# Full-width FFN, weight and angle products given out as four 32-column matmuls

## The chip, the core and the metric

The kernel runs on one core of a Trainium2 chip. A core has five engines with queues of their own: TensorE (PE, matrix products, with its weight loads shown as PEld), VectorE (DVE), ScalarE (ACT), GpSimd (POOL) and SyncE (SP, which here only issues DMAs). Each engine takes its instructions in the order of the program and waits on semaphores where it needs another's result. The metric is device time in microseconds, lower is better. All data are 32-bit floats.

## What is computed

A gated linear recurrence per head, and then a feed-forward block whose hidden layer is the largest of three products:

```python
for t in range(S):                                    # S = 768, B = 4, H = 8, D = 48
    S_re, S_im = ar*S_re - ai*S_im + kv, ar*S_im + ai*S_re
    y[:, :, t] = np.einsum('bhd,bhde->bhe', q[:, :, t], S_re)
x = y.transpose(0, 2, 1, 3).reshape(3072, 384)
h = np.maximum(np.maximum(x @ w1, x @ w2), x @ w3)    # w1..w3: 384 x 768
return h @ w_out                                      # w_out: 768 x 384
```

`ar` and `ai` are the gates `a_re` and `a_im` after they are scaled to a magnitude of at most 0.999.

## The kernel before

The 3072 rows are 24 blocks `x` of 128 steps; a group `g` (0 to 11) holds two of them, x and y, one of each of two batches. For each group the kernel works out the gates with logarithms (`gates`), sums angles along time with a triangular matrix (`cs`), sums logarithms (`sums`, `F`), turns k and q, transposes them (`tp`), forms scores (`A`, `B`), the state (`dk`), and outputs (`y`). The outputs of a group are the moving operand of the FFN: first three products by w1, w2, w3 (`up` for a whole group, 256 rows at a time; `up_one` for one block of the first two), then the product by w_out (`op`). For whole groups that last product is built from seven smaller ones, a Strassen scheme (`seven`), with 192 moving columns each, and two products with 384 (`Px`, `Py`). `project` makes it in the plain way for the first two blocks. `product` multiplies two weight matrices once, near the start (`wm`).

The whole order of work is written out by hand in the string `SCHEDULE`: a word such as `U11:3` or `P5:4` names a step and a group, and `Bound` (line 201 is its call) ties each instruction of an engine behind the engine's previous one. So the profile gives line 201 for nearly everything, and tiles are told apart by their names. No scheduler moves anything. PSUM is used as four pairs of banks, which the string `SLOTS` shares out in turn.

Every matrix product is `lhsT` (stationary, its columns become output partitions) by `rhs` (moving, its columns are streamed). In the trace each product of the program stands as two pairs of weight load and matmul (a transpose as one pair): 5,436 products of the program, 786 of them transposes, are the 10,086 matmuls of the profile. What part of the array a product takes is its shape, rows by columns:

- 128 x 128: `up`, `op` (from `up`, `up_one`, `seven`, `project`), `wm`, and, untouched by the change, `wt` and `pw` near the start.
- 128 x 64: `cs`, two products side by side on two column halves.
- 128 x 32: `A`, `B` and `y`, four side by side on the four column quarters (A and B use 112 of the rows).
- 64 x 64: `dk`, `F`, `sums`. 64 rows by 128: `tp`.

The products of one shape that follow each other are called a block below.

The calls that matter, before the change: `mm(out=ps[:, j], lhsT=ws[i][:, d, b*P:(b+1)*P], rhs=features(g)[:, ...])` in `up` (128 stationary columns, 256 moving), the same with `factor(i)` in `seven` (192 moving), `wx[:, 0]` for `Px`, `Py` and `wo`, `wp` in `project` (384 moving).

Of the kernel before, what the change touches and what calls it, by code (L numbers as in the profile page):

```python
# [139 lines left out]
def kernel(  # L140
# [15 lines left out]
    P = 128  # L156
    L64 = 64
# [30 lines left out]
    T = {}  # L188
# [18 lines left out]

    pe, dve, act, pool, sp = (Bound(e) for e in (nc.tensor, nc.vector, nc.scalar, nc.gpsimd, nc.sync))
    mm = pe.matmul

    def banks(nm, n=None):

# [182 lines left out]
    def every(view, j):  # L395

        return view.rearrange("p (i u d) -> p i u d", u=2, d=D)[:, :, j]
# [55 lines left out]
    def product(name, f):  # L453

        third = (vbs[2].rearrange("p c i d -> p (c i d)"), vbs[3].rearrange("p c i d -> p (c i d)"),
                 us["k"][2].rearrange("p h d -> p (h d)"))[f][:, 0:2 * DM]
        if name == "T":
            ps = T["wt", f] = banks("wt", 2 * DM)
            for u in range(2):
                for d in range(KD):  # L460
                    o = u * DM + d * P
                    pe.transpose(out=ps[:, o:o + P], in_=ws[0][:, d, (2 * f + u) * P:(2 * f + u + 1) * P], identity=ident)
        elif name == "t":
            act.copy(out=third, in_=T["wt", f])
        elif name == "M":
            for d in range(KD):
                ps = once(("wm", d // 2), lambda: banks("wm"))[:, d % 2, 0:DM]
                for u in range(2):
                    mm(out=ps, lhsT=third[:, u * DM + d * P:u * DM + (d + 1) * P], rhs=wo[:, 2 * f + u],
                       start=2 * f + u == 0, stop=2 * f + u == KF - 1)  # L470
        elif f < 2:
            n = 2 - f
            activation(out=wp[:, 2 * f:2 * f + n], in_=T["wm", f][:, 0:n, 0:DM], func=AF.Copy, scale=-1.0)
# [108 lines left out]
    def angles(g, c, name):  # L582

        x = g * C + c
        if name == "cs":
            ps = T["cs", x] = banks("cs", DM)
            for ch in range(2):
                for j in range(2):
                    dst, m = ps[j * L64:(j + 1) * L64, ch * HC:(ch + 1) * HC], slice(ch * L64, (ch + 1) * L64)
                    mm(out=dst, lhsT=upto[:, m], rhs=every(T["w", g][:, c * DM:(c + 1) * DM], j), start=True, stop=True)  # L590
        elif name == "t":
            T["t", x] = turned["t"][c]
            activation(out=T["t", x], in_=T["cs", x], func=AF.Copy, scale=-1.0, bias=MAGIC)
        elif name == "nf":
            T["nf", x] = turned["nf"][c]
            dve.scalar_tensor_tensor(out=T["nf", x], in0=T["t", x], scalar=MAGIC, in1=T["cs", x],
                                     op0=OP.subtract, op1=OP.add)
        elif name == "Cd":
            if (g + 1) % NS > 0:
                t = flat(T["ar", g + 1])[0:1]  # L600
                for j in range(2):
                    last = (j + 1) * L64
                    pool.dma_start(out=every(t[:, c * DM:(c + 1) * DM], j), accum_op=OP.add,
                                   in_=T["nf", x][last - 1:last, HC:].rearrange("p (i d) -> p i d", d=D))
        elif name == "af":
            T["af", x] = turned["t"][c]
            magnitude(T["af", x], T["nf", x])
        elif name in ("sa", "sb"):
            CS = T["CS", x] = css[c]
            if name == "sa":  # L610
                activation(out=CS[:, :, 0], in_=hv(T["af", x]), func=AF.Sin, scale=TWOPI, bias=-0.5 * math.pi)
            else:
                activation(out=CS[:, :, 1], in_=hv(T["nf", x]), func=AF.Sin, scale=TWOPI)
        else:
            return False
        return True
# [214 lines left out]
    def features(g):  # L831

        return xhx[:, 0:KD] if g % 2 == 0 else xhx[:, KD + KF:]
# [3 lines left out]
    def up_one(key, f, i, name):  # L837

        if name == "U":
            ps = T["up1", key, f, i] = banks("up", 2 * P).rearrange("p (f t) -> p f t", t=P)  # L840
            for j in range(2):
                for d in range(KD):
                    mm(out=ps[:, j], lhsT=ws[i][:, d, (f * 2 + j) * P:(f * 2 + j + 1) * P],
                       rhs=T["xT", key][:, d], start=(d == 0), stop=(d == KD - 1))
            return
        ps = T["up1", key, f, i]
        hT = once(("hT", key), lambda: ld2.tile([P, KF, P], FP, tag="ar", name="hT"))
        larger(hT[:, f * 2:(f + 1) * 2], ps, i)
# [9 lines left out]
    def up(g, f, i, name):  # L858

        if name == "U":  # L860
            ps = T["up", g, f, i] = banks("up", 3 * TG).rearrange("p (f t) -> p f t", t=TG)
            for j in range(3):
                b = ALONG[g % 2][3 * f + j]
                for d in range(KD):
                    mm(out=ps[:, j], lhsT=ws[i][:, d, b * P:(b + 1) * P],
                       rhs=features(g)[:, (d + 2 * (g % 2)) % KD], start=(d == 0), stop=(d == KD - 1))
        else:
            larger(xhx[:, KD + 3 * f:KD + 3 * f + 3], T["up", g, f, i], i)

# [23 lines left out]
    def seven(g, name):  # L893

        a11, a12, a21, a22 = (split(c, half, g) for c in range(2) for half in range(2))
        s1, s2, s3 = (sums[:, i] for i in range(3))
        if name in ("S1", "S2", "S3", "S4"):
            out, in0, in1, op = {"1": (s1, a21, a22, OP.add), "2": (s2, s1, a11, OP.subtract),
                                 "3": (s3, a11, a21, OP.subtract), "4": (s1, a12, s2, OP.subtract)}[name[1]]
            dve.tensor_tensor(out=out, in0=in0, in1=in1, op=op)  # L900
            return
        if name in ("P1", "P5", "P6", "P7", "r1", "r6", "r75", "r57"):
            ps = once(("seven", g), lambda: banks("op"))
            r = {1: ps[:, 0, 0:NH], 6: ps[:, 0, NH:DM], 5: ps[:, 1, 0:NH], 7: ps[:, 1, NH:DM]}
        else:
            ps = once(("op7", g), lambda: banks("op"))
            r = {2: ps[:, 0, 0:NH], 3: ps[:, 0, NH:DM], 4: ps[:, 1, 0:NH]}
        if name[0] == "P" and name[1:].isdigit():
            i = int(name[1:])
            left = {1: a11, 2: a12, 3: s1, 4: a22, 5: s1, 6: s2, 7: s3}[i]  # L910
            for n in range(4):
                mm(out=r[i], lhsT=left[:, n], rhs=factor(i)[:, (n + 2 * (g % 2)) % 4],
                   start=i in (1, 5, 6, 7) and n == 0, stop=i != 2 and n == 3)
        elif name in ("Px", "Py"):
            c = "xy".index(name[1])
            x0 = features(g)[:, 2 * (g % 2), c * P:(c + 1) * P]
            mm(out=ps[:, c, 0:DM], lhsT=x0, rhs=wx[:, 0], start=True, stop=False)
        else:
            ot = ots
            xl, xr, yl, yr = (ot[:, c, h * NH:(h + 1) * NH] for c in range(C) for h in range(2))  # L920
            if name == "r1":
                act.copy(out=xl, in_=r[1])
            else:
                if name == "r75":
                    two_ = ot.rearrange("p c n -> p (c n)")[:, NH:3 * NH].rearrange("p (u n) -> p u n", u=2)
                    again = yl.rearrange("p (u n) -> p u n", u=1).to_broadcast([P, 2, NH])
                    dve.tensor_tensor(out=two_, in0=again, in1=ps[:, 1, 0:DM].rearrange("p (u n) -> p u n", u=2), op=OP.add)
                    return
                out, in0, in1 = {"r6": (yl, xl, r.get(6)), "r57": (yr, yl, r.get(5)),
                                 "ox": (ot[:, 0], ot[:, 0], ps[:, 0, 0:DM]),  # L930
                                 "oy": (ot[:, 1], ot[:, 1], ps[:, 1, 0:DM])}[name]
                for n in (slice(NH, DM), slice(0, NH)) if name == "oy" and g == NG - 1 else (slice(None),):
                    dve.tensor_tensor(out=out[:, n], in0=in0[:, n], in1=in1[:, n], op=OP.add)

    def project(x, name):

        if name == "O":
            ps = T["op", x] = banks("op", DM)
            for d in range(KD):
                mm(out=ps, lhsT=T["xT", x][:, d], rhs=wp[:, d], start=(d == 0), stop=False)  # L940
            for f in range(KF):
                mm(out=ps, lhsT=T["hT", x][:, f], rhs=wo[:, f], start=False, stop=(f == KF - 1))
        elif name == "o":
            act.copy(out=ots[:, x % C], in_=T["op", x])
        elif name == "D":
# [97 lines left out]
```

## Time and profile before

| what | value |
|---|---|
| time, median of 3 runs | 559.99 us (558.49 to 560.16) |
| profiled execution: span, first to last instruction | 553.2 us |
| PE busy | 523.6 us (95%), 10,086 matmuls |
| DVE busy | 482.1 us (87%) |
| ACT busy | 368.2 us (67%) |
| POOL busy | 70.8 us (13%) |
| mean granted TensorE clock | 0.992 |

The profile gives for each engine the busy time, and for a group of instructions its count, its busy time, the mean duration of one and the idle time before it. A matmul's duration holds its way through the array, and matmuls overlap, so durations do not add up; what a matmul costs is the step from one to the next. The chain of waits follows the work back from the last instruction: each piece is the time from the end of the piece before it to its own end, with the number of instructions in it. For PE such a piece is what the block added to the end.

### The profile page before, as it was taken

The numbers are of one execution on the slowest core, as the hardware profiler recorded it, in microseconds if no ns is written. First come the engines' busy times: TensorE is split into PE (matmuls) and PEld (weight loads), VectorE is DVE, ScalarE is ACT, GpSimd is POOL, SyncE is SP. The second block draws the span as 40 slices with busy tenths as digits, with TensorE's granted clock in tenths as the row PEclk, the third lists the DMA queues.
The fourth block names the chain that finished last, engine by engine and source line by source line (L and its number), as shares of the span: only waits on it lengthen the run. The fifth ranks groups of instructions, "written<-read, shape, count | busy, mean of one in ns | idle before, by whom it ended". The sixth has DMA issues, their size and how long they took to land.

```text
span 553.2 us, 22687 instructions
## 1 busy us (share of the span) xinstructions
PE 523.6 (95%) x10086; PEld 448.1 (81%) x10086; DVE 482.1 (87%) x752; ACT 368.2 (67%) x653; POOL 70.8 (13%) x113
## 2 busy tenths in 40 slices
PE   2669799999999999999999999999999999999996
PEld 1355697788888888888988988988988988898985
DVE  4999999999999997999988888999999998887432
ACT  7999987777867787868776768786637835520100
POOL 7224140030020020000210200120020020000000
PEclk9979999999999999999999999999999999999999
DMA  8989774262616332324353245542361153000000
GB/s 203 295 246 176 174 131 79 50 128 63 109 38 124 67 68 51 61 44 88 72 121 58 35 85 108 101 91 54 62 125 20 32 105 72 2 31 2 31 1 28
DMA packets 141953, 47.51 MB, mean 86 GB/s; under 512 B 130464, under 2 KB 135584, under 8 KB 141856
## 3 DMA queue, kind: packets, MB, share of 16 engines
q1 hardware_dynamic: 136272, 37.77, 31.5%
q0 software_dynamic: 5584, 8.30, 8.9%
q8 instruction: 79, 1.29, 1.0%
q14 instruction: 18, 0.15, 0.1%
HBM read 33.03 MB, written 4.72 MB: 68 GB/s over the span
## 4 chain that ended last, share of the span: by engine, by line
PE 84%; DVE 7%; ACT 4%; SPq 2%; issue 1%; DMA 1%; DVEq 0%; ACTq 0%
PE up L201 33%; PE op L201 24%; PE y L201 7%; PE A L201 5%; PE tp L201 4%; PE dk L201 3%; PE sums L201 2%; PE cs L201 2%; DVE w L201 2%; SPq L201 2%; PE F L201 2%; PE B L201 1%; DMA wo<-in_moe_w_dram 1%; DVE atm L201 1%; ACT f L201 1%
## 5 line engine op out<-in xcount | busy, mean ns | idle before, releaser
L201 PE MATMUL up<-xhx,w 128*128 128x256 f32 x792 | 177.0, 382 | 0.1
L201 PEld LDWEIGHTS up<-xhx,w 128*128 128x128 f32 x792 | 148.6, 190 | 21.5 <-PE B L201 0.3
L201 ACT ACT_TABLE_LOAD x49 | 62.9, 1283 | 1.6 <-PEq L1027 0.8
L201 ACT COPY atm<-B 32x128 f32<-32x128 f32 x96 | 24.6, 256 | 37.8 <-DVE atm L201 19.7
L201 PE MATMUL op<-wo,xhx 128*128 128x192 f32 (+1 forms) x220 | 48.4, 363 | 0.0
L201 DVE TENSOR_TENSOR Q<-Q,f 112x1024 f32<-112x1024 f32 (+1 forms) x48 | 45.4, 952 | 1.7 <-ACT Q L201 1.2
L201 POOL DMA_DIRECT2D ar<-nf x40 | 34.6, 1305 | 60.3 <-DVE ar L201 48.9
L201 ACT ACTIVATE f<-F 48x232 f32<-48x232 f32 x96 | 34.5, 359 | 10.1 <-PE F L201 6.1
L201 PEld LDWEIGHTS op<-wo,xhx 128*128 128x128 f32 x220 | 36.5, 190 | 4.6 <-issue 0.6
L201 PE MATMUL y<-atm,vb 128*32 128x64 f32 x1152 | 39.0, 221 | 0.2 <-ACT K L201 0.2
L201 PE MATMUL y<-QG,g 112*32 112x64 f32 x1408 | 38.0, 219 | 0.2 <-issue 0.2
L201 PEld LDWEIGHTS y<-atm,vb 128*32 128x32 f32 x1152 | 32.4, 109 | 5.3 <-issue 2.9
L201 PEld LDWEIGHTS y<-QG,g 112*32 112x32 f32 x1408 | 34.8, 109 | 0.3 <-issue 0.3
L201 DVE TENSOR_TENSOR ot<-ot,op 128x384 f32<-128x384 f32 (+1 forms) x56 | 25.6, 464 | 10.7 <-PE op L201 6.4
L201 PE MATMUL op<-wo,strassen 128*128 128x192 f32 x176 | 33.0, 331 | 0.0
L201 POOL DMA_DIRECT2D Ln<-e x9 | 8.3, 923 | 192.2 <-ACT e L201 53.8
L201 PE MATMUL A<-Q,K 112*32 112x80 f32 x1536 | 31.6, 234 | 1.4 <-DVE Q L201 1.4
L201 DVE COPY_PREDICATED atm<-masko,A 128x256 f32<-128x256 uint8 x72 | 31.2, 435 | 1.7
L201 PE MATMUL op<-w,strassen 128*128 128x192 f32 x176 | 32.2, 329 | 0.0
L201 PEld LDWEIGHTS A<-Q,K 112*32 112x32 f32 x1536 | 27.3, 110 | 4.2 <-issue 3.1
L201 PEld LDWEIGHTS op<-wo,strassen 128*128 128x128 f32 x176 | 28.8, 190 | 0.8
L201 ACT COPY Q<-tp 112x1024 f32<-112x1024 f32 x22 | 22.3, 1014 | 10.7 <-PE tp L201 10.5
(148 smaller groups left out, 1080.5 us busy)
## 6 DMA issues: line engine op xcount, KB each, us to landing
ar<-in_a_re_dram SPq DMA_DIRECT2D x24, 192.0 KB, 3.1
ai<-in_a_im_dram SPq DMA_DIRECT2D x24, 192.0 KB, 3.5
q<-in_q_dram SPq DMA_DIRECT2D x96, 48.0 KB, 2.6
k<-in_k_dram SPq DMA_DIRECT2D x96, 48.0 KB, 2.6
vb<-in_v_dram SPq DMA_DIRECT2D x96, 48.0 KB, 3.0
out_dram<-ot SPq DMA_DIRECT2D x23, 192.0 KB, 2.6
Ln<-e POOLq DMA_DIRECT2D x9, 384.0 KB, 4.1
w<-L POOLq DMA_DIRECT2D x7, 384.0 KB, 4.4
```

Source lines behind the costliest of these rows:

```text
L201: ins = f(*a, **kw)
```

## The change

A helper `mmq` gives a product out as four, one for each quarter of 32 stationary columns, with the same moving operand. `up`, `up_one`, `seven` (`P1` to `P7`, `Px`, `Py`), `project` and the weight product in `product` call it in place of `mm`. `cs` goes from two 64-column products per half to four with 32 columns. What is computed, the order of the steps, the tiles, and the instructions of the other engines stay as they are. SP's DMAs keep their order; three loads of v wait for one more semaphore of PE or ACT than before.

```diff
+    def mmq(out, lhsT, rhs, **kw):
+
+        for o in range(0, P, 32):
+            mm(out=out[o:o + 32], lhsT=lhsT[:, o:o + 32], rhs=rhs, **kw)
...
-                    mm(out=ps, lhsT=third[:, u * DM + d * P:u * DM + (d + 1) * P], rhs=wo[:, 2 * f + u],
-                       start=2 * f + u == 0, stop=2 * f + u == KF - 1)
+                    mmq(out=ps, lhsT=third[:, u * DM + d * P:u * DM + (d + 1) * P], rhs=wo[:, 2 * f + u],
+                        start=2 * f + u == 0, stop=2 * f + u == KF - 1)
...
-                for j in range(2):
-                    dst, m = ps[j * L64:(j + 1) * L64, ch * HC:(ch + 1) * HC], slice(ch * L64, (ch + 1) * L64)
-                    mm(out=dst, lhsT=upto[:, m], rhs=every(T["w", g][:, c * DM:(c + 1) * DM], j), start=True, stop=True)
+                for o in range(0, P, 32):
+                    dst, m = ps[o:o + 32, ch * HC:(ch + 1) * HC], ch * L64 + o % L64
+                    mm(out=dst, lhsT=upto[:, m:m + 32], rhs=every(T["w", g][:, c * DM:(c + 1) * DM], o // L64),
+                       start=True, stop=True)
...
-                    mm(out=ps[:, j], lhsT=ws[i][:, d, b * P:(b + 1) * P],
-                       rhs=features(g)[:, (d + 2 * (g % 2)) % KD], start=(d == 0), stop=(d == KD - 1))
+                    mmq(out=ps[:, j], lhsT=ws[i][:, d, b * P:(b + 1) * P],
+                        rhs=features(g)[:, (d + 2 * (g % 2)) % KD], start=(d == 0), stop=(d == KD - 1))
...
-                mm(out=r[i], lhsT=left[:, n], rhs=factor(i)[:, (n + 2 * (g % 2)) % 4],
-                   start=i in (1, 5, 6, 7) and n == 0, stop=i != 2 and n == 3)
+                mmq(out=r[i], lhsT=left[:, n], rhs=factor(i)[:, (n + 2 * (g % 2)) % 4],
+                    start=i in (1, 5, 6, 7) and n == 0, stop=i != 2 and n == 3)
...
-            mm(out=ps[:, c, 0:DM], lhsT=x0, rhs=wx[:, 0], start=True, stop=False)
+            mmq(out=ps[:, c, 0:DM], lhsT=x0, rhs=wx[:, 0], start=True, stop=False)
...
-                mm(out=ps, lhsT=T["xT", x][:, d], rhs=wp[:, d], start=(d == 0), stop=False)
+                mmq(out=ps, lhsT=T["xT", x][:, d], rhs=wp[:, d], start=(d == 0), stop=False)
             for f in range(KF):
-                mm(out=ps, lhsT=T["hT", x][:, f], rhs=wo[:, f], start=False, stop=(f == KF - 1))
+                mmq(out=ps, lhsT=T["hT", x][:, f], rhs=wo[:, f], start=False, stop=(f == KF - 1))
```

`up_one` is changed as `up` is. The program has 834 full-width products (396 and 72 `up` with 256 and 128 moving columns, 308 and 40 `op` with 192 and 384, 18 `wm` with 384) that become 3,336, and 96 `cs` that become 192: 2,598 products more, or 5,196 matmuls and as many weight loads in the trace.

More of the change, by code (lines that the diff above doesn't have):

```diff
@@ L842, in up_one @@
                 for d in range(KD):
-                    mm(out=ps[:, j], lhsT=ws[i][:, d, (f * 2 + j) * P:(f * 2 + j + 1) * P],
-                       rhs=T["xT", key][:, d], start=(d == 0), stop=(d == KD - 1))
+                    mmq(out=ps[:, j], lhsT=ws[i][:, d, (f * 2 + j) * P:(f * 2 + j + 1) * P],
+                        rhs=T["xT", key][:, d], start=(d == 0), stop=(d == KD - 1))
             return
```

## The prediction

> **What bounds the kernel now.** I read the busy times and the chain of waits on the page first.
>
> ```profile
> span 553.2 us, 22687 instructions
> PE 523.6 (95%) x10086; PEld 448.1 (81%) x10086; DVE 482.1 (87%) x752; ACT 368.2 (67%) x653; POOL 70.8 (13%) x113
> ...
> PE 84%; DVE 7%; ACT 4%; SPq 2%; issue 1%; DMA 1%; DVEq 0%; ACTq 0%
> PE up L201 33%; PE op L201 24%; PE y L201 7%; PE A L201 5%; PE tp L201 4%; PE dk L201 3%; PE sums L201 2%; PE cs L201 2%; DVE w L201 2%; SPq L201 2%; PE F L201 2%; PE B L201 1%; DMA wo<-in_moe_w_dram 1%; DVE atm L201 1%; ACT f L201 1%
> ```
>
> TensorE ends the kernel: 84% of the chain is its work, 59% of the span `up`, `op` and `cs`, the products that the change touches. The question is what a block of products costs PE. The chain in order of time tells it, since a piece is the time from the end of the block before to the block's own end:
>
> ```profile
> 59.49 1.75 DVE Q L201 x2
> 61.37 1.35 PE A L201 x64
> ...
> 116.39 4.08 PE up L201 x18
> ...
> 158.60 11.85 PE up L201 x54
> ...
> 263.04 2.80 PE op L201 x16
> ...
> 385.59 1.50 PE op L201 x8
> ```
>
> Up to about 62 us, while loads and gates are made, the chain runs through DVE and ACT (the `Q` of DVE above is the end of that); behind it 94% of the pieces' time are PE's, by the same view from 62 us on:
>
> ```profile
> by line: PE up L201 37.2%; PE op L201 26.8%; PE y L201 7.8%; PE A L201 5.4%; PE tp L201 4.4%; PE dk L201 3.8%; PE sums L201 2.7%; PE cs L201 2.6%; PE F L201 1.7%; PE B L201 1.7%; DVE atm L201 0.7%; issue 0.6%; DVE w L201 0.6%; ACT f L201 0.
> ```
>
> Thirty-six matmuls more of `up` take 11.85 - 4.08 = 7.77 us, so a step is 215.8 ns with 256 moving columns. Eight more of `op` take 1.30 us, a step of 162.5 ns with 192 columns. The difference, 53.3 ns for 64 columns, makes 0.833 ns a column. But 18 steps of 215.8 ns are 3.88 us, and the piece has 4.08; 8 steps of 162.5 ns are 1.30, and the piece has 1.50. Each full-width block, whatever its length, costs 0.20 us beyond its stream. That is what the change can remove.
>
> The same subtraction for the narrow shapes:
>
> ```profile
> 85.36 0.80 PE cs L201 x8
> ...
> 121.52 1.25 PE A L201 x64
> ...
> 127.65 0.39 PE B L201 x32
> 128.04 1.15 PE A L201 x64
> ...
> 139.37 1.45 PE cs L201 x16
> ...
> 186.49 1.73 PE y L201 x112
> 188.22 1.11 PE A L201 x64
> ```
>
> `cs`: eight more take 0.65 us, 162.5 ns for each two side by side, and 0.80 - 0.65 = 0.15 us go on the block itself. `A`, four side by side with 80 columns: 64 take 1.11 us right behind `y`, which has the same shape, so 69 ns for four, and 1.25 us behind `tp`, another shape. So coming from another shape costs 0.14 us, coming from the same shape nothing. This is the main reading: the 0.20 and 0.15 us are paid for the change of shape, not for the block.
>
> **The change part by part.** *The stream.* A full-width matmul with 80 columns would take 162.5 - 112 x 0.833 = 69.2 ns by the steps above. Four matmuls of `A` on the quarters take 69 ns. A `cs` pair with 192 columns takes 162.5 ns, as one `op` matmul with 192. So the fours and pairs that the trace has run side by side without loss, and I cost four quarters in place of one full width at nothing. [...] The trace shows no quarter with more than 80 columns, so the price has bounds. Below, 0: a four has the same columns to stream, and nothing in the rows streams faster. Above, the worst row of a four, `y`:
>
> ```profile
> 71.51 1.27 PE y L201 x80
> ```
>
> Against 1.73 us for 112, 32 more take 0.46 us, 57.5 ns for four; a full-width matmul with 64 columns would take 162.5 - 128 x 0.833 = 55.8. These 1.7 ns, paid by each of the 1,668 fours that replace full-width matmuls (834 products, two matmuls each), are 2.8 us. I take 0, because `A`, with 80 columns nearer to 128 to 384, shows 0; 2.8 us stay for the range.
>
> *The blocks.* In the program's order TensorE changes shape 189 times before and 119 times after. Of 61 full-width blocks 56 vanish into 128 x 32 ones (`wt` and `pw` stay), of 14 `cs` blocks all; the number of 128 x 32 blocks stays at 52, since those that merge are as many as the new ones that stand alone between `tp`, `dk`, `F` or `sums`. So 56 x 0.20 + 14 x 0.15 = 13.2 us (11.1 with 0.198 from the `up` and `op` rows, and 2.1) leave PE's queue.
>
> *The borders with B.* [...] The new program has 25 borders of B with changed products. Bounds: 0 each, as between `y` and `A`, or 0.044 each, 1.1 us. I take 1.1, since B is one side of all of them. That leaves 12.1 us.
>
> *Other queues.* DVE, ACT and POOL issue what they issued. SP's three loads of v that wait for one more semaphore queue loads behind them, but the v load lies a group ahead; I cost this at nothing, and it is covered by PE's work on the group before. The longer program must be fetched:
>
> ```profile
> q8 instruction: 79, 1.29, 1.0%
> ```
>
> 1.29 MB are the 20,172 loads and matmuls of PE at 64 bytes. There are 10,392 more, 41 fetches more of 256 each. In `y` and `A` PE already goes through 128 to 224 of them in 1.1 to 1.7 us; in a changed `up` 8 go in 215.8 ns, 37 in a us, a third of that rate. So I cost it at nothing as well.
>
> *What of it reaches the end.* Before 62 us PE waits for gates and weights, and the four vanishing blocks there (0.65 us) give nothing. That leaves 11.45 us over the 492 us behind, 2.3%. PE's inputs come from DVE and ACT, and how much room DVE has is read from its busy time by stretch:
>
> ```profile
> 62.00:100.00 38.00, 37.38 (x61) 1.00 0.59 111
> 100.00:150.00 50.00, 48.48 (x76) 1.00 0.44 85
> 150.00:200.00 50.00, 47.36 (x74) 1.00 0.39 73
> 200.00:350.00 150.00, 133.01 (x206) 1.00 0.40 77
> 350.00:450.00 100.00, 95.78 (x148) 1.00 0.36 70
> 450.00:505.00 55.00, 46.41 (x68) 1.00 0.17 36
> 505.00:554.00 49.00, 20.08 (x34) 0.98 0.05 17
> ```
>
> The columns are the stretch, its length and DVE's busy time. From 200 to 350 and behind 450 us DVE is idle for 11%, 16% and 59%, and of DVE's waits the longest are for PE itself:
>
> ```profile
> DVE xhx L201 <- PE up L201: 19.8, 12, 7.2
> ...
> DVE ot L201 <- PE op L201: 6.4, 5, 2.5
> ```
>
> They shrink as PE gets ahead. There, over 254 us, I let nine tenths of 2.33% through: 5.3 us. From 62 to 200 and 350 to 450 us DVE is idle for 1.6 to 5.3%, partly behind ACT. PE can gain 2.33% there only where DVE's idle time is PE's doing, and what it does not get through turns into waits of PE for `atm`, `nf`, `Q` or `xhx`, which are late next. I take half over 238 us: 2.8 us. The sum is 8.1 us: 553.2 becomes 545.1 us. The median of the runs is 560.0, 6.8 us above the profiled span, for what lies around it; with that, 551.9 us.
>
> [...]
>
> **The rivals.** *All of it comes through.* If the waits for DVE are slack enough, PE's 12.1 to 13.2 us come off whole: 547.9 to 546.8 us. For it: the 84% of the chain. Against: DVE's 37.38 of 38 and 48.48 of 50 us.
>
> *The gain is swallowed.* The schedule was ordered so tightly that DVE and ACT, not PE, set the pace once PE is 2% faster; PE then waits where it had changed shape. 558.5 to 560. For it: the stretches with 95% and more. Against: from 505 us on PE works with DVE at 20.08 of 49 us, and the chain's 84%.
>
> *The price of shape stays.* If a change of rows (112 in `A`, `B` and half of `y`, 128 in the changed products) costs what a change of columns does, little vanishes: 560 to 562.8, with the 2.8 us from above. Against it: `y` mixes both row counts, and `A` behind it costs nothing.
>
> *Slower: giving out a matmul costs TensorE more than its share of the stream.* A four with 192 columns leaves 162.5 / 4 = 40.6 ns for each load and matmul, with 256 columns 54, with 128 columns 27. From 41 ns on the 308 products of `op` lengthen. At 49 ns, four times the 12.2 that `B`'s row bounds it to (0.39 us for 32), 308 x (392 - 325) are 20.6 us, the 72 `up` with 128 columns 12.5, `cs` 3.2: 36 us, about 592 when some 4 us of the gain in blocks are set against them. For it: no row has a quarter with 192 columns. Against: `B`'s 12.2 ns. [...]
>
> **How the numbers follow.** The gain as summed, with some part of it swallowed: 0.73; all through: 0.12; swallowed: 0.06; the price of shape stays: 0.03; slower: 0.06. The likeliest gives 551.9. With all costs at their good end, 13.2 us whole, it is 546.8; with 2.8 and 1.1 us off and only a third of the rest through, 557. I widen by half a microsecond or a little more on each side, because the runs of before differ by 1.7 us: 546 to 557.5. A change of 0.3%, 1.7 us, is about what a measurement can tell. Faster by more than that are the first two cases, 0.85; within it the third and fourth, 0.09; slower 0.06.
>
> **What would show it.** `up` x18 between other shapes in the chain at about 4.02 us as 72, and less where it follows `A` or `y` (3.9); eight matmuls of `op` as 32 right behind `y` at 1.30 in place of 1.50; `A` behind `up` at 1.11 in place of 1.25. PE's waits for DVE and ACT should grow by some 4 us, most of them from 62 to 200 and 350 to 450 us. The prediction is wrong if the four of `up` has a step above 216 ns (the stream), if the pieces still hold 0.20 us beyond it (the shape), or if the pieces shrink and PE's waits grow by as much (the inputs).

## The result and the profile after

The changed kernel takes 592.74 us (median of 4 runs, 590.79 to 596.05), the kernel before beside it 559.38 us: 1.062 times the time, interval 1.057 to 1.066. It is slower, and the prediction was wrong. The page of the changed kernel, its busy times, the queue that fetches instructions, and the engines' shares of the chain:

```profile
span 590.3 us, 33082 instructions
...
PE 527.6 (89%) x15282; PEld 408.3 (69%) x15282; DVE 483.7 (82%) x752; ACT 368.4 (62%) x653; POOL 70.0 (12%) x113
...
q8 instruction: 119, 1.95, 1.4%
...
PE 81%; issue 6%; DVE 4%; SPq 4%; DMA 3%; ACT 1%; DVEq 0%; ACTq 0%
```

TensorE works hardly longer (527.6 us against 523.6), but the span grows by 37.1 us, and the chain holds 6% of "issue" where it held 1%: time in which PE stands still and no other engine is seen to release it. The waits of PE (us in all, times, longest), first of the changed kernel and then the only such row of the kernel before:

```profile
PE y L201 <- issue: 8.5, 7, 1.5
PE up L201 <- issue: 5.2, 5, 1.9
PE F L201 <- issue: 5.1, 4, 2.1
PE B L201 <- issue: 4.4, 3, 2.0
PE op L201 <- issue: 3.1, 4, 1.2
...
PE A L201 <- issue: 2.7, 2, 1.7
```

```profile
PE y L201 <- issue: 0.2, 1, 0.2
```

The pauses stand before products of every kind, `y` and `F` among them, which the change does not touch. The steps and blocks look much as predicted, when the chain is read between the pauses:

```profile
128.54 1.68 issue
...
130.68 4.02 PE up L201 x72
...
135.74 1.24 PE A L201 x64
136.99 3.89 PE up L201 x72
...
151.97 1.59 PE y L201 x112
```

72 matmuls of `up`, eighteen fours of 216 ns, take 3.89 us behind the same shape (`A`) and 4.02 behind another; `y` behind the same shape takes 1.59 us where it took 1.73. The fours stream as full-width matmuls do.

What the pauses wait for shows in their places. Counted through PE's program (loads, matmuls, semaphore instructions), all 30 stretches behind 62 us in which PE stands idle, more than 0.45 us from one matmul's start to the next, and that no other compute engine explains lie at one and the same remainder of the count by 256 (one of them, 0.5 us before `dk`, the view puts down to a load). And 256 is what one fetch brings: before, 79 packets moved 1.29 MB, 16 KB each, and 1.29 MB are 64 bytes for each of PE's 20,172 loads and matmuls, so a packet holds 256; now there are 119. The place in PE's program where one such block of 256 ends and the next begins is called a border below. One of the pauses, in the chain of the changed kernel:

```profile
201.64 1.52 PE y L201 x100
...
203.31 0.98 PE A L201 x56
...
204.43 0.45 PE op L201
204.88 1.24 issue
206.12 1.01 PE op L201 x9
```

And the DMA view of the stretch from 203.2 to 206.2 us, whose first line shows the busy share of the DMA engines in 40 slices:

```profile
DMA  9000000000000000000000009949986990994994
...
q8 instruction: 1, 0.02, 3.0%
```

The fetch is the first slice, at 203.26 us, and the view counts a packet's whole time where it starts: 3.0% of 16 engines over 3.0 us are 1.45 us, so this packet ends at 204.71. The other traffic, from 205 us on, is of one of the kernel's own queues. PE goes through `y` and `A`, 132 and 114 instructions in a us by the rows above, meets the border, stands from 204.88 us, and goes on at 206.12, 2.9 us after the fetch began and 1.4 us after its packet ended.

So it is each time. In the 16 profiled executions, at every pause that no engine's or other queue's work explains, PE goes on 2.2 to 3.2 us after a fetch began and 1.2 to 1.7 us after the end of its packet (2.22 to 2.86 and 1.26 to 1.64 in the changed kernel), and no border behind 62 us is passed sooner after its packet than 1.2 us. Fetches and borders keep step through every run, one fetch to each border. A packet takes 0.9 to 2.0 us (0.88 to 1.55 in the kernel before, 0.88 to 1.70 in the changed one), and no two fetches of any run begin closer together than 3.2 us (3.34 and 3.36 in these two). When a fetch begins is less regular: in the changed kernel half of them begin 0.8 to 1.5 us after the border before was passed, but over all runs it goes from 4.4 us before that to 5.0 us after it, and what sets the moment is not shown. Where work takes PE from one border to the next in less than some 3.4 us, about the 3.36 us between the two closest fetches of the changed kernel, it was likely to stand still. The 3.4 us, here and in the expectations below, are an estimate and no sharp rule. Of the 38 blocks of the changed kernel with less than 3.4 us of work, 27 end in a pause and 11 do not; three pauses stand behind blocks of up to 3.8 us; and the kernel before has four such blocks and no pause.

These 30 gaps, each less the 0.1 us that is allowed here for an ordinary step from start to start, are 37.3 us. The work that lay between 100 and 500 us before is 3.9 us shorter when product is compared with product and these gaps are cut out (5.1 when six smaller gaps at borders, of 0.2 to 0.45 us, are cut out as well). The other 3.7 us of the difference in span lie before 100 and behind 500 us. Some of them may be the clock (stretch, its length, DVE's busy time, granted clock, then the share of the DMA engines and GB/s):

```profile
50.00:75.00 25.00, 24.29 (x37) 0.93 0.82 173
75.00:100.00 25.00, 18.45 (x29) 0.93 0.49 81
```

It was 1.00 in both stretches before. PE is busy for 38.2 us of these 50 in the changed kernel; 0.07 of that are 2.7 us, an estimate.

### The profile page after: what moved, and what is told of

The parts are those of the page before. It is cut to its first block, busy times and chain, and to the rows that moved or that the text cites. A ratio compares the mean times of both kernels' runs of the same rounds, so it can differ in the third digit from the quotient of the medians.

```text
span 590.3 us, 33082 instructions
## 1 busy us (share of the span) xinstructions
PE 527.6 (89%) x15282; PEld 408.3 (69%) x15282; DVE 483.7 (82%) x752; ACT 368.4 (62%) x653; POOL 70.0 (12%) x113
## 4 chain that ended last, share of the span: by engine, by line
PE 81%; issue 6%; DVE 4%; SPq 4%; DMA 3%; ACT 1%; DVEq 0%; ACTq 0%
PE up L201 32%; PE op L201 22%; PE y L201 6%; PE A L201 5%; PE tp L201 4%; SPq L201 4%; PE dk L201 4%; PE cs L201 3%; PE sums L201 2%; DMA strassen<-in_moe_w_dram 2%; PE F L201 2%; PE B L201 1%; DMA q<-in_q_dram 1%; DVE w L201 1%; DVE atm L201 1%
## 5 line engine op out<-in xcount | busy, mean ns | idle before, releaser
L201 PE MATMUL up<-xhx,w 128*32 128x256 f32 x3168 | 178.1, 380 | 1.9 <-issue 1.7
L201 PEld LDWEIGHTS up<-xhx,w 128*32 128x32 f32 x3168 | 114.6, 110 | 55.6 <-issue 4.1
L201 PE MATMUL op<-wo,xhx 128*32 128x192 f32 (+1 forms) x880 | 53.3, 365 | 2.3 <-issue 2.3
L201 ACT COPY atm<-B 32x128 f32<-32x128 f32 x96 | 24.5, 256 | 40.7 <-PE B L201 20.8
L201 PE MATMUL y<-atm,vb 128*32 128x64 f32 x1152 | 40.7, 221 | 4.5 <-issue 4.4
L201 PE MATMUL y<-QG,g 112*32 112x64 f32 x1408 | 40.2, 219 | 4.1 <-issue 4.1
L201 PEld LDWEIGHTS op<-wo,xhx 128*32 128x32 f32 x880 | 34.8, 111 | 10.4 <-issue 7.0
L201 PEld LDWEIGHTS y<-atm,vb 128*32 128x32 f32 x1152 | 35.2, 110 | 7.4 <-issue 4.7
L201 PE MATMUL op<-w,strassen 128*32 128x192 f32 x704 | 35.7, 331 | 0.8 <-issue 0.8
L201 PE MATMUL op<-wo,strassen 128*32 128x192 f32 x704 | 36.0, 327 | 0.0
L201 ACT COPY ot<-op 128x192 f32<-128x192 f32 (+1 forms) x13 | 4.5, 344 | 44.3 <-PE op L201 44.2
```

The lines of the kernel that those rows point to most:

```text
L201: ins = f(*a, **kw)
```

## The experiments

None leaves out a part of the computation; a product that is given out several times is only computed again. "Pauses" are the gaps at borders of 256 behind 62 us in the profiled run, counted and summed as above; the instructions are PE's. Each ratio is to the kernel before on the same chip, where that took 556.25 to 559.38 us; differences in the text are to it as well. The pauses of `e7_after_plus192` are those of an execution of 592.36 us.

| kernel | instructions | pauses, us | time, us | ratio, interval |
|---|---|---|---|---|
| before | 20,312 | 0 | 559.38 | 1 |
| changed | 30,704 | 30, 37.3 | 592.74 | 1.062, 1.057 to 1.066 |
| e1_after_shift | 30,832 | 31, 32.1 | 586.36 | 1.051, 1.045 to 1.057 |
| e2_before_A9 | 21,336 | 4, 5.5 | 570.49 | 1.023, 1.017 to 1.028 |
| e3_op_only | 24,488 | 21, 20.8 | 577.76 | 1.034, 1.026 to 1.042 |
| e3_up_only | 25,928 | 15, 18.1 | 573.89 | 1.028, 1.023 to 1.034 |
| e4_halves | 23,648 | 15, 17.4 | 571.85 | 1.027, 1.021 to 1.032 |
| e1_before_shift | 20,440 | 20, 22.0 | 577.92 | 1.039, 1.033 to 1.045 |
| e5_up_long | 20,384 | 11, 11.1 | 573.47 | 1.031, 1.024 to 1.037 |
| e6_cs_only | 20,696 | 16, 15.3 | 572.26 | 1.028, 1.023 to 1.032 |
| e7_before_plus256 | 20,568 | 1, 0.7 | 558.02 | 1.003, 1.000 to 1.006 |
| e7_before_plus64 | 20,376 | 17, 17.7 | 571.77 | 1.026, 1.020 to 1.032 |
| e7_after_plus64 | 30,768 | 30, 34.0 | 586.07 | 1.051, 1.043 to 1.058 |
| e7_after_plus192 | 30,896 | 29, 35.1 | 590.54 | 1.055, 1.046 to 1.065 |
| e8_placed | 23,396 | 5, 4.3 | 560.78 | 1.009, 1.005 to 1.012 |
| e8_placed_shift | 23,524 | 21, 24.5 | 579.79 | 1.042, 1.037 to 1.048 |

**Are the pauses tied to products or to places?** `e1_after_shift` is the changed kernel with the first angle-cut products given out three times, at 10 to 12 us, where TensorE waits anyway:

```diff
-            for i in range(2):
+            for i in [0, 1] * (3 if x == 0 else 1):
```

> The changed kernel, with the 16 products F of the very first block given out three times in place of once (the same values written again), while TensorE still waits for its first inputs: 128 loads and matmuls more near the start, everything behind them 128 places later in TensorE's program. Theory (supply): TensorE's program comes in blocks of 256 instructions, a block is in use no sooner than about 3.4 us after the one before was entered, and TensorE stands still at the border when it went through the block faster. Then the stalls stay on the borders of 256 but move to other products: of the 30 products at which the changed kernel stood still for more than 0.45 us behind 62 us, fewer than a third stand still again. The time stays within 8 us of 592.7 on either side, as other stretches fall between two borders. Rival (place): the stalls belong to certain products, where inputs or a queue are late. Then the same products stall and the time is 592.7 plus at most 0.5.

Measured 586.36 us. The 31 pauses have moved: none stands at one of the 30 products that paused before, and each stands again at the one remainder by 256. In the chain of this kernel, around the place shown above, the outputs and scores pause in the middle, and the `op` behind them does not:

```profile
201.64 1.59 PE y L201 x112
203.22 0.09 PE A L201 x3
203.31 0.33 issue
203.65 1.24 PE A L201 x59
...
204.95 3.81 PE op L201 x74
```

So the place in the program decides. The sum of the pauses changes with it as well, by 5 us.

**Does untouched work pause when it is long enough?** `e2_before_A9` is the kernel before, with the scores of the first block of group 6 given out nine times: 1,024 instructions more (not the 1,536 that a later expectation names), at 115 in a us.

```diff
-            for h in range(H):
+            for h in list(range(H)) * (9 if x == 12 else 1):
```

> The kernel before, with the score product A of one block (group 6, x) given out nine times in place of once, the same values each time: 512 matmuls and 512 loads more in the 128x32 shape, no change of shape, nothing else touched. By the stream of A (69 ns for four) they take 128 x 0.069 = 8.9 us. Rival (the stream alone counts): the time grows by 8.9 us and the block shows no pause. Theory (supply): nine A are 1,152 instructions, four to five blocks of 256, each at least 3.4 us: 13.6 to 17 us in place of 10, so the time grows by 13 to 16 us, and A shows pauses of some 1.2 us exactly 256 instructions apart.

Measured 570.49 us, 12.4 more than before, where the stream alone is eight times 1.11, 8.9. (Stream and pauses make 14.4; the interval of the ratio allows 9.7 to 15.7.) The chain of this kernel:

```profile
285.98 1.78 PE A L201 x91
287.76 1.16 issue
288.92 2.42 PE A L201 x128
291.34 1.59 issue
292.93 2.42 PE A L201 x128
295.34 1.86 issue
297.20 3.19 PE A L201 x128
300.39 0.26 issue
```

Between the pauses stand 128 matmuls, with their 128 loads one fetch, and from one end of a pause to the next it is 4.0, 4.3 and 3.5 us. That is the supply in this stretch: 256 instructions in 3.5 to 4.3 us, 60 to 74 in a us. Nowhere else does this kernel pause: 1,024 is four times 256, and the later borders fall where they fell.

**Which part of the change pays?** `e3_op_only` and `e3_up_only` leave all else as before:

```diff
+    def mmq(out, lhsT, rhs, **kw):
+
+        for o in range(0, P, 32):
+            mm(out=out[o:o + 32], lhsT=lhsT[:, o:o + 32], rhs=rhs, **kw)
...
```

with `mmq` called in `project` and `seven` alone, or in `up` and `up_one` alone. The weight product, 216 of the 10,392 instructions, has no variant of its own.

> Only the products by w_out (seven and project) are given out as fours; up, cs and the weight product are as before. 4,176 loads and matmuls more, 30 changes of shape fewer, worth 5.6 us on TensorE. Theory (supply): stalls on borders of 256 instructions where op stands next to y, A and B, some 8 to 15 us of them, so the time is 2 to 10 us above before (562 to 570). Rival (the fours are good and something else in the change, up or cs or the v loads, costs the 33 us): 4 us below before, 555 to 556.

> Only up and up_one are given out as fours; op, cs and the weight product are as before. 5,616 loads and matmuls more, 18 changes of shape fewer, worth 4.0 us on TensorE. With 37 instructions a microsecond up itself is half as dense as the supply of 256 per 3.4 us (75). Theory (supply): up no longer gives the queue its long rest of 9 instructions a microsecond, so blocks that hold y, A, tp, F or dk stall: 6 to 14 us of stalls, 561 to 570 us. Rival (the fours are good, op or cs cost the 33 us): 3 us below before, 556 to 557.

Measured 577.76 and 573.89 us, both above what either theory gave. `e6_cs_only` has the angle sums alone in quarters, in the way of the change:

> Only the angle sums in quarters (four 32-column matmuls in place of two 64-column ones), everything else as before: 384 PE instructions more. With the weight product (a few products) it is what the two parts measured leave of the change. Supply theory: the added instructions are few, but each sum now gives out its instructions twice as fast beside the scores and outputs, and all later borders shift: 0 to 6 us of pauses, less some 1 to 2 us of shape changes saved: 558 to 564. Rival 'the price is that of the converted products, and parts add': the whole, 33.4, less 18.4 for the output part and 14.5 for the up part leaves 0.5: 559 to 561, without pauses.

Measured 572.26 us, a miss again: 384 instructions more cost 14.5 us. The three parts cost 19.7, 15.8 and 14.5 us, 50 together, and the whole change 33.4. They do not add, and the price has little to do with the number of instructions.

**Number or shape?** `e4_halves` gives the products of `mmq` out as two of 64 columns, the angle sums as before:

```diff
+        for o in range(0, P, 64):
+            mm(out=out[o:o + 64], lhsT=lhsT[:, o:o + 64], rhs=rhs, **kw)
```

> The FFN, output and weight products of the kernel before in two matmuls on 64-column halves of the array instead of four on quarters; the angle sums as before. 3,336 PE instructions more (23,648) instead of 10,392. Supply theory (256 instructions cannot follow each other in less than some 3.4 us): a dense block gives out half as many instructions per us as with quarters, so PE's queue still runs ahead and asks for the next fetch before the border; fewer and smaller pauses than in either half of the change (18 to 21 us there), 3 to 10 us in all, all of them at one place of every 256 of the stream; the shape changes stay or nearly so: 561 to 569. Rival 'each matmul given out has a price': 33.4 us over 10,392 instructions is 3.2 ns each, here 10.7 us spread over all the products and without pauses: 570. Rival 'it is the 32-column shape that costs': no change, 558 to 560.

Measured 571.85 us, above the theory's range and near the rival's 570. But the 14 us are not spread over the products, as that rival has it: they are 15 pauses, 17.4 us, each at a border.

**Was the kernel before lucky?** `e1_before_shift` is the kernel before with the edit of `e1_after_shift`.

> The kernel before with the angle-cut products of the first block given out three times, as in the shifted changed kernel: 128 instructions more at about 30 us, nothing else. Every later border of 256 instructions falls on other products. Supply theory: before, the closest border had its fetch 2.38 us ahead, just enough; shifted by half a block some borders will be later than that, 0 to 5 pauses, 0 to 4 us in all: 559 to 563. Rival 'the position of the borders does not matter': only the products themselves, under 0.5 us, 558 to 559.5.

Measured 577.92 us. I had expected 0 to 4 us of pauses, and there are 22.0. Nothing is changed but 128 instructions at a time when PE waits. One place of it in the chain, and the same products in the kernel before:

```profile
223.94 1.25 PE A L201 x64
225.19 0.10 PE B L201 x10
225.29 0.89 issue
226.18 0.39 PE B L201 x19
226.57 4.08 PE up L201 x18
```

```profile
212.69 1.25 PE A L201 x64
213.94 0.34 PE B L201 x29
214.27 0.03 issue
214.31 4.12 PE up L201 x18
```

Between the same scores `A` and the same `up`, PE pauses for 0.89 us in the one and not in the other. The kernel before has the same dense runs, of `y`, `A` and `B`, but its borders fall so that each has its fetch begun in time: 2.38 us ahead at the closest, which is just enough.

`e5_up_long` repeats one full-width step of group 6, as much stream as in `e2_before_A9` with 72 instructions:

```diff
-            for j in range(3):
+            for j in list(range(3)) * (3 if (g, f, i) == (6, 1, 1) else 1):
```

> The kernel before with one up-projection step of group 6 (nine full-width products of 256 columns, a block of about 3.9 us) given out three times: 7.8 us more of TensorE's stream, but only 72 instructions, against 8.9 us in 1,536 instructions where the scores of group 6 were given out nine times (which cost 12.4). Supply theory: the stream and nothing more, plus or minus 1 us for the shifted borders: 566 to 568 beside a kernel before at 559. Rival 'stream put into this stage costs 1.4 times its length, because something else in the stage is late behind it': 10.9 us, 569 to 571.

Measured 573.47 us, 15.7 more; both ranges miss. The block itself is as the stream says:

```profile
288.29 11.85 PE up L201 x54
```

7.8 us more than the 4.08 of 18, without a pause. The rest lies in 11.1 us of pauses, eight of the eleven behind 340 us, where the borders are shifted by 72. (7.8 and 11.1 are 18.9, more than the 15.7; what takes up the other 3 was not separated.) The three others, 1.6 us together, stand at 101, 105 and 198 us, ahead of the edit, where the program is that of the kernel before. There the same borders were passed 2.4 to 3.0 us after their fetches began, among the closest of that kernel, without a gap that counts. So the place says which borders are close, and from one execution to the next a close one can turn into a short pause.

**Place alone.** More positions of both kernels, by giving the same products out two, four or five times:

> The kernel before with the angle-cut products of the first block given out five times: exactly 256 instructions more (at 9 to 12 us, where TensorE waits anyway), so every later border of 256 instructions falls on the same products as in the kernel before. Theory 'it is where the borders fall that decides': no pauses, within 2 us of the kernel before (557 to 561), though it is given out 128 instructions longer than the shifted kernel at 577.9. Rival 'more instructions, or repeating these products, cost something of their own': twice what 128 more did, some 590 to 600, or at least as much, 578.

> The kernel before with the first angle-cut products given out twice: 64 instructions more, borders shifted by a quarter of a fetch. Theory 'position decides': borders now fall elsewhere in the short dense runs of scores and outputs; between the kernel before (no pauses) and the one shifted by 128 (22 us of pauses): 5 to 20 us, 563 to 578. Rival 'only the shift by 128 was unlucky': 557 to 560.

> The changed kernel with the same 64 instructions more. Theory 'position decides, and the changed kernel has more dense runs': pauses at other products, 25 to 40 us in all, 580 to 597, with no phase near the kernel before. Rival 'the change itself costs little and has only met a bad position': with another position it can come as low as the shape changes say, 548 to 565.

> The changed kernel with 192 instructions more, the fourth quarter of a fetch. As for 64: position decides and the dense runs are more, 580 to 597; rival 548 to 565. The mean over the four positions (592.7, 586.4 and these two) beside the mean over positions of the kernel before says what the change costs apart from where the borders fall: more by 5 to 20 us if the extra fetches cost something themselves, less by some 10 us if only the position did it.

With 256 more, all borders are back on their products, and the kernel takes 558.02 us, 1.003 of the kernel before. Its one row is at the border that was the closest in the kernel before:

```profile
PE y L201 <- issue: 0.6, 1, 0.6
```

With 64 it takes 571.77, with 128 577.92. So it is the border, not the number and not the repeated products. The changed kernel takes 592.7, 586.1, 586.4 and 590.5 us at its four positions, 588.9 on the mean; that is 28 to 34 us above the kernel before on the same chip, 31 on the mean, and none is near it. (The kernel before was not shifted by 192.)

**Number or place, once more.** What remained open was whether the added instructions have a price of their own, some 13 us between these 31 and the 18 that the two shifted kernels before lie above their base on the mean (15.5 and 20.1). `e8_placed` gives out in quarters only what stands in 54 steps of the schedule, nearly as many instructions more as the halves have, chosen by a fit to the pauses measured until then so that no border comes early (the fit is an estimate: it gave 37 us of pauses for the changed kernel, where 37.3 were measured, and 21 for the kernel before with 128 instructions more, where 22.0 were):

```diff
+        n = 32 if T["word"] in PLACED else P
+        for o in range(0, P, n):
+            mm(out=out[o:o + n], lhsT=lhsT[:, o:o + n], rhs=rhs, **kw)
```

> [...] Theory 'where the borders fall decides, not how many there are': 553 to 559 beside a kernel before at 556 to 559, pauses under 2 us. Rival 'each further fetch, or each matmul given out, has its price' (halves: 14 us for 3,336 more): some 570.

> The same kernel with the first angle-cut products given out three times: 128 instructions more in 23,524, and every later border on other products. Theory 'place decides': 23 us of pauses by the fitted model, 574 to 584. Rival 'the number decides': as without the shift, within 2 us.

Measured 560.78 and 579.79 us. The first is 4.0 us above the kernel before, outside the expected range by some 2 us and far from the rival's 570; its pauses are 4.3 us, one of them 1.6:

```profile
PE F L207 <- issue: 1.5, 1, 1.5
...
PE y L207 <- issue: 1.1, 2, 0.8
...
PE B L207 <- issue: 0.5, 1, 0.5
PE op L207 <- issue: 0.4, 1, 0.4
```

(Line 207 is line 201 of the others.) The second has 128 instructions more and takes 19.0 us more; its pauses are 24.5 us, where the fit gave 23. 3,084 instructions more cost 4 us in one place, and with 128 on top of them 23 in another: the place of the borders decides. That the number works through it, since more and longer dense runs leave fewer places that are good, fits the four positions of the changed kernel and is argued, not shown.

No version was found that beats the kernel before: `e8_placed` was chosen to save shape changes without pauses, and comes out 0.9% slower.

## Why the prediction was wrong

*The step that failed* is the fetch of the longer program: "In `y` and `A` PE already goes through 128 to 224 of them in 1.1 to 1.7 us; in a changed `up` 8 go in 215.8 ns, 37 in a us, a third of that rate. So I cost it at nothing as well." The two rates are right, and the inference is not. 128 and 224 instructions are less than the 256 of one fetch, and such a run says nothing of the supply beyond it. `e2_before_A9` measured that: 256 in 3.5 to 4.3 us. The changed `up`, 37 in a us, stays under it, but `op` with 192 columns gives out 8 in 162.5 ns, 49 in a us, and `y`, `A` and `B` beside them more than 110. Full-width work between the dense runs, 9 instructions in a us, made most blocks of 256 last long; in quarters the same work takes a quarter of its time for each instruction, and in 30 places the fetch comes later than PE. The page's row of 79 fetches stood in the prediction; their distance from each other and from the borders was not looked at.

*The step that was missing* is that the kernel before has its place. 10,392 instructions more move every border, and a move by 64, 72 or 128 costs the kernel before 8 to 20 us. By the runs, each against the kernel before on its own chip, of the 33.4 us some 18 are this (the mean of 15.5 and 20.1 for shifts by 64 and 128), 13 the more and longer dense runs (31 on the mean of the changed kernel's four positions), and 2 the changed kernel's own position. This is an estimate: other shifts of the kernel before would cost it less or more.

*The stream* was right: fours of `up` at 216 ns and of `op` at 162, as one full-width matmul. The upper end of 2.8 us was not needed.

*The blocks* were right in kind and too large: 12.1 us off PE, 11.45 of them behind 62 us, are 9.3 for the 400 us between 100 and 500. Measured there: 3.9, or 5.1 with the smaller gaps cut out too. What became of the other 4 to 5 was not separated. The 1.1 us taken off in it for borders with `B` are 25 times 0.044, the difference of two rows of the kernel before, `A` in 1.15 us behind `B` and in 1.11 behind `y`; what causes it is not shown. In four places of the changed kernel `op` right behind `B` takes 5.85, 9.13, 3.94 and 3.94 us (72, 208, 80 and 96 matmuls) where it took 6.00, 9.29, 4.09 and 4.10: 0.15 or 0.16 less, so that some 0.04 of the 0.20 stay.

*What of it reaches the end* was not put to the test. PE got later, not ahead, and DVE waited longer for it instead (for `up`, 23.9 us against 19.8). The waits of PE for DVE and ACT that I had growing by 4 us stayed as they were: 25.4 us in all before, 26.1 now.

*From span to time* I added 6.8 us for what lies around the span. The later profiled runs have their own time only 2 to 3 us above their span, so the profiled execution of 553.2 us was some 4 us shorter than the runs whose median is 560.0. This decides nothing here.

*The slower rival* named 592, and the time was 592.7, but for another reason. It had each four lengthened by what giving out costs; no four is longer. The number agrees by chance.

## What to carry to other kernels

An edit that splits matmuls is to be costed in instructions as well as in stream: count PE's loads and matmuls over every stretch of 256, at its own step, and see whether it lasts the 3.4 us estimated here; where it does not, a pause is likely (27 of 38 such stretches in this kernel), not certain. When a kernel of this density gets even a few instructions more or fewer, all later borders move, so a variant and its base should each be timed at several positions (here 64, 128, 192 and 256 instructions at an idle moment) before a gain or a loss is put down to the edit. In the traces here PE's waits for "issue" at one remainder by 256 of its program were the sign.

## What was not expected of the hardware

A shift of 64 instructions, given out while TensorE waits, costs 15.5 us 60 to 500 us later, and one of 256 costs nothing that shows (558.02 against 556.25 us on the same chip, interval of the ratio from 1.000). A fetch's packet takes 0.9 to 2.0 us, yet PE goes on only 1.2 to 1.7 us after its end; what fills that time no trace here shows. In one place it is shown not to be contention with the kernel's own transfers. From 546 to 549 us of the changed kernel the fetch is the only packet that moves on the core's queues, 1.9% of 16 engines over 3 us, 0.9 us, beginning at 546.3 us, and PE stands still all the same:

```profile
q8 instruction: 1, 0.02, 1.9%
```

```profile
546.51 0.26 PE B L201 x28
546.77 2.01 issue
548.77 0.22 PE B L201 x2
```

It goes on 2.4 us after the fetch began and 1.5 us after the packet's end, as elsewhere.
